# Decode of two attention and two MLP layers on one core: four streaming tasks in each window, ten behind it, and the chain's LayerNorms in fewer steps

## The chip, the core and the metric

The kernel runs on one core of one Trainium2 chip, as one launch. The metric is the device time in microseconds. A kernel is timed in several runs, and the median counts. A profile is taken of one further execution. Its own time and its span (first to last instruction) are given beside the median, because every duration below comes from that one execution. Engines are named as in the profile: PE (TensorE matmuls), PEld (its weight loads), DVE (VectorE), ACT (ScalarE), POOL (GpSimd) and SP (SyncE, which issues the loads here).

## The reference

Eight sequences (B = 8) decode one token each. A layer is attention over a cache of 8192 keys, with 32 query heads on 8 key/value heads of 128 elements, followed by an MLP of 512 x 1792. The same layer, with the same caches and weights, is applied twice.

```python
def _A_ref(x, k_cache, v_cache, wq, wo):
    q = (lambda x, *d: x.transpose(*d))((x @ wq).reshape(B, Sq, Hq, Dh), 0, 2, 1, 3)
    k = jnp.repeat(k_cache, rep, axis=1)
    v = jnp.repeat(v_cache, rep, axis=1)
    scores = jnp.einsum("bhqd,bhkd->bhqk", q, k) * (Dh ** -0.5)
    p = _softmax(scores, axis=-1)
    o = jnp.einsum("bhqk,bhkd->bhqd", p, v)
    return (lambda x, *d: x.transpose(*d))(o, 0, 2, 1, 3).reshape(B, Sq, Hq * Dh) @ wo
...
x = x + _A_ref(_layernorm(x, axis=-1), A_k_cache, A_v_cache, A_wq, A_wo)
x = x + _B_ref(_layernorm(x, axis=-1), B_w1, B_w2)
x = x + _A_ref(_layernorm(x, axis=-1), A_k_cache, A_v_cache, A_wq, A_wo)
x = x + _B_ref(_layernorm(x, axis=-1), B_w1, B_w2)
```

## The kernel before

**Tasks and granules.** A task is one key/value head of one sequence in one layer, (layer, b, g): 128 tasks. A task has four granules (`SPT`) of 2048 keys. For each granule one 512 KB load brings K and one brings V into the arena, which has 28 slots (`NSLOT`) of 512 KB. In iteration c of the main loop the kernel works on granule c. It transposes K on PE in two halves (L545), and ACT (L554) and DVE (L556) copy the halves back. It then computes the scores (L579). The product with V (L639) runs `LAG` = 6 granules later. The softmax is spread over the iterations by c modulo 4: `softmax_max` (DVE L590 and L592, POOL L594) at the end of iterations with remainder 3; `softmax_exp` (DVE L599 and L601, ACT L603) and then `softmax_sum` (DVE L609, POOL L611) in those with remainder 0 and 1; `emit_pt` (L619, L623) with remainder 1; the reciprocal (L628) with remainder 2.

**Kept heads.** The last 20 granules of K of a sequence (`KEEP`: heads 3 to 7) stay transposed in the arena from the first layer to the second, as do 3 granules of V (`KEEPV`); one granule of K is parked in PSUM. So a second-layer task of heads 3 to 7 loads V alone and transposes nothing. Heads 0 to 2 are free: they stream K and V in both layers.

**The order of the tasks** is laid by `make_tasks`. For each sequence b it takes the five kept heads of the first layer (`kept[b]`), then a window of free tasks (other sequences' heads 0 to 2, from `ahead` for the first layer and `behind` for the second), then the five kept heads of the second layer (`c[b]`), and at once `kept[b + 1]`. The windows have 6, 5, 5, 5, 5, 5, 5 and 6 tasks, 42 in all. From the end of `kept[b]` to `c[b]` the held K and V leave few slots for streaming.

**The loads.** `plan_loads` sorts all loads by the half step at which they are needed and gives each a slot and the half step after which that slot is free (`after`). SP issues them in that order, each when its slot has been released, by the scores for K (L579) or by the product with V (L639). Two neighbouring granules of a kept head are loaded as one 1 MB transfer if two neighbouring slots are free early enough. Before there are 199 such pairs and 442 single transfers, 641 in all.

**The chain.** When the last kept head of the first layer has been normalised, `chain_of(b)` lists what leads to the second layer's queries: the residual and first LayerNorm, the MLP, the second LayerNorm and the projection with `wq`. Its steps run one by one inside the iterations, at three places of the loop body: MID (after the copies of the transposed halves and the softmax steps, ahead of the product with V), TILE (PE work just ahead of the scores; in an iteration of a free task this comes after MID) and TURN (after the scores, ahead of `softmax_max`). At each place at most one step runs, and only if it is the next one and of that kind. The engines run their instructions in the order in which they are issued.

**A LayerNorm of the chain** has four parts in `ln_stages`. The first sums on DVE (L661) and across partitions on POOL (L663). The second (L669, L689, L690, POOL L692) sums the squares. The third (L708, L710, L698, L703) starts the reciprocal root. The fourth (L698, L703, L717) finishes it and writes the normalised column that PE reads next. In the chain the second and third are MID steps and the fourth is a TURN step, so that second, third with fourth, and the PE step behind them stand in three successive iterations.

In what follows w0, w1, ... are the granules of a window, counted from its first. As `LAG` is 6, the chain's first step comes in w6, whose remainder is 2. The chain before is: w6 `add_rest` and `met` (residual and first part), w7 second, w8 third and fourth, w9 `up`, w10 `expo` and `silu`, w11 and w12 `down`, w12 `gained` (residual and first part), w13 second, w14 third and fourth, w15 to w18 the queries (`ask` twice and `answer`, two times).

Of the kernel before, what the change touches and what calls it, by code (L numbers as in the profile page):

```python
# [17 lines left out]
KEEP = 20  # L18
KEEPV = 3
PARK = 1  # L20
LAG = 6
WIDE = 8
AHEAD = 8
# [114 lines left out]
def make_tasks(nb, nkv, keep_from):  # L138


    first = int(keep_from)
    a = [[(0, b, g) for g in range(first)] for b in range(nb)]
    kept = [[(0, b, g) for g in range(first, nkv)] for b in range(nb)]
    c = [[(1, b, g) for g in range(first, nkv)] for b in range(nb)]
    d = [[(1, b, g) for g in range(first)] for b in range(nb)]
    ahead = [t for b in range(1, nb) for t in a[b]]
    behind = []
    tasks = a[0] + kept[0]
    na = 0
    for b in range(nb):  # L150
        if b:
            tasks += kept[b]
        size = -(-(2 * first * (nb - 1)) // nb) if b in (0, nb - 1) else 2 * first * (nb - 1) // nb
        must = max(0, first * min(b + 1, nb - 1) - na)
        nd = size if b == nb - 1 else min(len(behind), first, size - must)
        tasks += behind[:nd]
        del behind[:nd]
        take = ahead[na:na + size - nd]
        na += len(take)
        tasks += take  # L160
        if b + 1 == nb:
            tasks += behind
        tasks += c[b]
        behind += d[b]
    tasks += d[nb - 1]
    assert na == len(ahead)
    return tasks

# [5 lines left out]
def plan_loads(tasks, kept, parked, keptv, nslot, ngran):  # L174

    single = set()
    while True:
        loads, copies = lay_loads(tasks, kept, parked, keptv, nslot, ngran, single)
        double = {rows_of(d, kept) for d in loads if d.n == 2}
        torn = {rows_of(d, kept) for d in loads if d.n == 1} & double  # L180
        if not torn:
            return loads, copies, double
        single |= torn
# [10 lines left out]
def lay_loads(tasks, kept, parked, keptv, nslot, ngran, single):  # L194
# [4 lines left out]
    for i, (layer, b, g) in enumerate(tasks):  # L199
        for k in range(ngran):  # L200
# [6 lines left out]
            if layer == 0 or (g, k) not in keptv:  # L207
                last = i if layer or (g, k) not in keptv else at[(1, b, g)]
                wanted.append(Load("V", layer, b, g, k, 2 * (c + LAG), 2 * (last * SPT + k + LAG)))
    wanted.sort(key=lambda d: (d.need, d.kind))  # L210
# [46 lines left out]
def _build(ctx, nc, A_x, A_k_cache, A_v_cache, A_wq, A_wo, B_w1, B_w2, out):  # L257
    B, _sq, D = A_x.shape
# [3 lines left out]
    REP = HQ // HKV  # L262
    KT = D // 128
# [9 lines left out]
    tasks = make_tasks(B, HKV, (len(order) - KEEP) // NGRAN)  # L273
    assert len(tasks) == 2 * B * HKV
    task_at = {t: i for i, t in enumerate(tasks)}
    parked = set(order[len(order) - PARK:])
    loads, copies, wide = plan_loads(tasks, kept, parked, keptv, NSLOT, NGRAN)
# [62 lines left out]
    mxp, nb, rs = [[few(1) for _ in range(NST)] for _ in range(3)]  # L340
# [27 lines left out]
    MISC = ps_bank("MISC")  # L368
    assert PARK == 1
    KEPTp = [ps_bank("KEPTp", BF16) for _ in range(HALVES)]  # L370
# [61 lines left out]
    with nc.Block() as block:  # L432

        @block.sync
        def _(sync_eng):
# [346 lines left out]
                )  # L782

            TILE, MID, TURN = range(3)

            def chain_of(b):
                x0, x1, x2 = [XT[n][:, :, b:b + 1] for n in range(3)]
                xn = one[2]
                qt2, rq2 = QT2[b % 2], f"QT2_{b % 2}"

                def attended():
                    sum_rows(x1, "XT1", x0, "XT0", 1.0)

                def up():
                    tiles([(t, xn[:, k, :], across(w1_sb[:, k, :], 0, FT)[:, t], k == 0, k == KT - 1)
                           for k in range(KT) for t in range(NT)], ["w1", "xn1"])

                hv = MISC[:, 0:FT * QR:QR]

                def expo():  # L800
                    upright(FT)
                    op(act, lambda: act.activation(eh, hv, ACT.Tanh, scale=0.5), reads=["MISC"], writes=["eh"])

                def silu():
                    op(dve, lambda: dve.scalar_tensor_tensor(hsT, eh, 1.0, hv, op0=ALU.add, op1=ALU.mult),
                       reads=["MISC", "eh"], writes=["hsT"])

                def down(q0, q1):
                    def run():
                        tiles([(t, hsT[:, q:q + 1], across(w2_sb[:, q, :], 0, KT)[:, t], q == 0, q == FT - 1)  # L810
                               for q in range(q0, q1) for t in range(NT)], all_of("w2") + ["hsT"])
                    return run

                AC = KB // QR

                def ask(a, k0, k1):
                    def run():
                        tiles([(t, xn[:, k, :], across(wq_sb[:, k, :], a * AC, (a + 1) * AC)[:, t],
                                k == 0, k == KT - 1) for k in range(k0, k1) for t in range(NT)], ["wq", "xn1"])
                    return run  # L820

                def answer(a):
                    def run():
                        upright(AC)
                        op(dve, lambda: dve.tensor_copy(qt2[:, a * AC:(a + 1) * AC], MISC[:, 0:KB:QR]),
                           reads=["MISC"], writes=[rq2])
                    return run

                n1, n2 = ln_stages(x1, "XT1", 1, one), ln_stages(x2, "XT2", 1, one)

                def gained():
                    sum_rows(x2, "XT2", x1, "XT1", 0.5)
                    n2[0]()

                def met():
                    attended()
                    n1[0]()

                return (
                    [(TURN, met), (MID, n1[1]), (MID, n1[2]), (TURN, n1[3])]  # L840
                    + [(TILE, up), (MID, expo), (TURN, silu), (TILE, down(0, FT // 2)), (TILE, down(FT // 2, FT))]
                    + [(TURN, gained), (MID, n2[1]), (MID, n2[2]), (TURN, n2[3])]
                    + [x for a in range(HQ // AC)
                       for x in ((TILE, ask(a, 0, KT // 2)), (TILE, ask(a, KT // 2, KT)), (TURN, answer(a)))]
                )

            def closing(n):
# [58 lines left out]
            def add_rest(b):  # L906
                while heads[b]:
                    add_heads(b)
# [33 lines left out]
            emit_q(0)  # L942

            chain = []
            chain_b = [None]
            turn = [0]
            last0 = {b: max(task_at[(0, b, g)] for g in range(HKV)) for b in range(B)}
            first1 = {b: min(task_at[(1, b, g)] for g in range(HKV)) * SPT for b in range(B)}
# [1 line left out]
            first = min(g for g, _k in kept)  # L950
# [16 lines left out]

            for c in range(NC + LAG):
                if c < NC:
                    layer, b, g, k = where(c)  # L970
                if c and c % SPT == 0 and c < NC:
                    assert layer == 0 or not chain or chain_b[0] != b
                    emit_q(c // SPT)
                ready = c < NC and (c < AHEAD or layer == 1 and (g, k) in kept)
                if ready:
                    scores(c)
                t = c + LEAD if c >= late - LEAD else c
                if not ready or t >= late:
                    emit_t(t, 0)
                    emit_t(t, 1)  # L980
                soft(c - SPT, softmax_exp)
                soft(c - SPT - 1, softmax_sum)
                soft(c - SPT - 2, softmax_rcp)
                step(MID)
                if 0 <= c - LAG:
                    emit_pv(c - LAG)
                    if (c - LAG) % SPT == SPT - 1:
                        emit_norm((c - LAG) // SPT)
                while copies and copies[0].need <= 2 * c:
                    emit_unpark(copies.pop(0))  # L990
                issue_until(2 * c)
                soft(c - SPT - 1, emit_pt)
                if turn[0] == B and not chain and heads[B]:
                    add_heads(B)
                if c < NC and not ready:
                    scores(c)
                issue_until(2 * c + 1)
                step(TURN)
                soft(c - SPT + 1, softmax_max)
                if c >= LAG and (c - LAG) % SPT == SPT - 1:  # L1000
                    tj = (c - LAG) // SPT
                    layer, b, g = tasks[tj]
                    if layer == 0:
                        heads[b].append(g)
                    elif b == B - 1:
                        heads[B].append(g)
                    if layer == 0 and tj == last0[b]:
                        assert not chain and turn[0] == b
                        chain.extend([(TILE, lambda b=b: add_rest(b))] + chain_of(b))
                        chain_b[0] = b  # L1010
                        turn[0] = b + 1
            assert not queue and not chain

            rest = closing(B)
# [37 lines left out]
```

## Time and profile before

| what | value |
|---|---|
| median of 3 runs | 1140.38 us (1137.9 to 1142.65) |
| the profiled execution | 1136.29 us |
| its span | 1134.5 us |
| busy PE / PEld / DVE / ACT / POOL | 935.0 / 698.9 / 558.3 / 491.0 / 117.3 us |
| loaded from HBM | 452.47 MB, 399 GB/s over the span |
| DMA engines busy | 9 tenths or more in 39 of 40 slices |
| single 512 KB loads: issue to landing, median | K 7.2 us, V 6.6 us |
| paired 1 MB loads: issue to landing, median | K 20.1 us, V 13.8 us |
| mean granted TensorE clock | 0.926 |

How to read it: the page gives sums over the whole span. The stages of the order above follow each other eight times, and a stage is read with the view of windows, which gives for each stretch of time the busy time of the engines, the granted clock, the share of time in which the DMA engines were busy, and the bytes per second. The timeline lists instructions in order of time: start, duration, engine, line, what it writes and reads, and in brackets the idle time before it with what ended it.

### The profile page before, as it was taken

What the parts mean: (1) busy time and instruction counts of PE and PEld (TensorE: products, weight loads), DVE (VectorE), ACT (ScalarE), POOL (GpSimd) and SP (SyncE); (2) the same over time, 40 slices, a digit from 0 to 9 for tenths busy, and PEclk for the clock granted to TensorE, in tenths of its full rate; (3) what the DMA queues carried; (4) which work ended last, traced back from release to release, by engine and by line L of the source; (5) the groups of instructions that cost most, each with busy time, mean ns of one, the idle gap of its engine ahead of it and who ended that gap; (6) DMA issues with size and microseconds to landing.
All of it is one profiled execution on the core that took longest, in us unless ns stands there. A gap on an engine that the chain in (4) does not pass through costs nothing.

```text
span 1134.5 us, 42794 instructions
## 1 busy us (share of the span) xinstructions
PE 935.0 (82%) x18792; PEld 698.9 (62%) x18792; DVE 558.3 (49%) x1710; ACT 491.0 (43%) x778; POOL 117.3 (10%) x300
## 2 busy tenths in 40 slices
PE   6687887888888888888888888888878888888796
PEld 4366664666566665666567665676566655665565
DVE  6444554445534553446444553446444553455444
ACT  5354442455335542554245542554245432554332
POOL 0000111001100101001100111001100111011010
PEclk9699998999879997999889997999789997999888
DMA  9999999999999999999999999999999999999995
GB/s 376 413 413 415 392 407 412 420 411 385 405 419 416 391 408 417 419 411 392 412 419 415 394 403 418 418 403 393 407 419 411 381 408 419 417 388 367 396 420 224
DMA packets 95550, 455.26 MB, mean 401 GB/s; under 512 B 10620, under 2 KB 10884, under 8 KB 69380
## 3 DMA queue, kind: packets, MB, share of 16 engines
q1 hardware_dynamic: 95348, 452.51, 99.1%
q8 instruction: 148, 2.42, 0.9%
q14 instruction: 38, 0.31, 0.1%
q10 hardware_dynamic: 16, 0.01, 0.0%
HBM read 452.47 MB, written 0.01 MB: 399 GB/s over the span
## 4 chain that ended last, share of the span: by engine, by line
DMA 40%; PE 37%; DVE 11%; ACT 5%; issue 5%; SPq 2%; POOL 0%; POOLq 0%; ACTq 0%; DVEq 0%
DMA arena<-in_A_v_cache_dram 32%; PE TPp L545 18%; PE SCp L579 9%; DVE arena L556 9%; DMA arena<-in_A_k_cache_dram 7%; PE OTp L639 4%; ACT arena L554 4%; PE TPp L619 2%; DMA wq<-in_A_wq_dram 2%; SPq L401 2%; PE MISC L754 2%; ACT P L603 1%; PE KEPTp L545 1%; DVE small L628 1%; DVE small L599 0%
## 5 line engine op out<-in xcount | busy, mean ns | idle before, releaser
L554 ACT COPY arena<-TPp 128x1024 bf16<-128x1024 bf16 x344 | 348.1, 1012 | 393.1 <-PE TPp L545 389.7
L545 PE MATMUL TPp<-ident,arena 128*128 128x128 bf16 x5504 | 377.8, 223 | 28.1 <-DMA arena<-in_A_k_cache_dram 22.3
L556 DVE COPY arena<-TPp 128x1024 bf16<-128x1024 bf16 x344 | 238.0, 692 | 329.7 <-PE TPp L545 327.0
L545 PEld LDWEIGHTS TPp<-ident,arena 128*128 128x128 bf16 x5504 | 317.9, 100 | 118.1 <-issue 62.1
L639 PE MATMUL OTp<-PT,arena 128*128 128x32 bf16 x8192 | 292.0, 179 | 56.6 <-DMA arena<-in_A_v_cache_dram 52.7
L639 PEld LDWEIGHTS OTp<-PT,arena 128*128 128x128 bf16 x8192 | 252.6, 97 | 136.0 <-DMA arena<-in_A_v_cache_dram 105.7
L579 PE MATMUL SCp<-arena,QB 128*32 128x512 bf16 x2048 | 223.8, 429 | 71.5 <-DVE arena L556 24.0
L603 ACT ACTIVATE P<-SCp,small 128x512 bf16<-128x512 f32 x128 | 87.9, 687 | 203.5 <-DVE small L601 157.8
L590 DVE TENSOR_REDUCE small<-SCp 128x1 f32<-128x512 f32 x128 | 88.5, 692 | 103.7 <-PE SCp L579 102.5
L579 PEld LDWEIGHTS SCp<-arena,QB 128*32 128x32 bf16 x2048 | 59.8, 96 | 112.5 <-ACT arena L554 53.4
L594 POOL PARTITION_ALL_REDUCE small<-small x128 | 47.5, 371 | 620.9 <-DVE small L592 620.9
L611 POOL PARTITION_ALL_REDUCE small<-small x128 | 55.2, 431 | 332.4 <-DVE at L653 146.5
L619 PE MATMUL TPp<-ident,P 128*128 128x128 bf16 x512 | 54.9, 235 | 26.4 <-ACT arena L554 14.6
L619 PEld LDWEIGHTS TPp<-ident,P 128*128 128x128 bf16 x512 | 31.5, 103 | 35.5 <-ACT arena L554 20.1
L623 DVE COPY PT<-TPp 128x256 bf16<-128x256 bf16 x128 | 37.3, 291 | 20.8 <-PE TPp L619 18.9
L609 DVE TENSOR_SCALAR small<-small 128x4 f32<-128x4 f32 x128 | 28.7, 224 | 37.9 <-ACT P L603 37.9
L592 DVE TENSOR_SCALAR small<-small 128x4 f32<-128x4 f32 x128 | 29.4, 229 | 4.5
L599 DVE TENSOR_TENSOR small<-small 128x4 f32<-128x4 f32 x128 | 20.0, 157 | 20.9 <-POOL small L594 20.9
L767 DVE STREAM_TRANSPOSE MISC<-MISC 128x128 f32<-128x128 f32 (+2 forms) x40 | 22.1, 552 | 10.0 <-PE MISC L754 10.0
L754 PE MATMUL MISC<-wo,at 128*32 128x128 bf16 x1024 | 26.0, 231 | 0.0
L603 ACT ACTIVATION_READ_ACCUMULATOR P<-SCp,small 128x1 f32 x128 | 24.7, 193 | 0.0
L601 DVE TENSOR_REDUCE small<-small 128x1 f32<-128x4 f32 x128 | 20.1, 157 | 4.4
(102 smaller groups left out, 329.7 us busy)
## 6 DMA issues: line engine op xcount, KB each, us to landing
arena<-in_A_v_cache_dram SPq DMA_DIRECT2D x131, 1024.0 KB, 13.8
arena<-in_A_v_cache_dram SPq DMA_DIRECT2D x226, 512.0 KB, 6.6
arena<-in_A_k_cache_dram SPq DMA_DIRECT2D x216, 512.0 KB, 7.2
arena<-in_A_k_cache_dram SPq DMA_DIRECT2D x68, 1024.0 KB, 20.1
arena<-in_A_wo_dram SPq DMA_DIRECT2D x8, 512.0 KB, 12.7
wq<-in_A_wq_dram SPq DMA_DIRECT2D x1, 4096.0 KB, 24.8
w<-in_B_w_dram SPq DMA_DIRECT2D x1, 1792.0 KB, 22.3
arena<-in_B_w_dram SPq DMA_DIRECT2D x3, 512.0 KB, 16.9
```

The lines of the kernel that those rows point to most:

```text
L545: lambda c=c: pe.transpose(tpv[:, c, :], chunk(slot, h * GRP + c), ident[:, :])
L554: op(act, lambda: act.copy(dst, bank[:, :]), reads=[rt], writes=[r_half(slot, h)])
L556: op(dve, lambda: dve.tensor_copy(dst, bank[:, :]), reads=[rt], writes=[r_half(slot, h)])
L579: lambda t=t: pe.matmul(SCp[bank][t * QR:(t + 1) * QR, :], QB[qn][:, NGRAN - 1 - k:NGRAN - 1 - k + QR], keys[:, t * KB:(t + 1) * KB], star ...
L590: op(dve, lambda: dve.tensor_reduce(mxp[st][:, :], SCp[bank][:, :], AX.X, ALU.max), reads=[f"SC{bank}"], writes=[f"mxp{st}"])
L594: op(pool, lambda: pool.partition_all_reduce(mxa[st][:, :], mxr[st][:, :], 128, bass.bass_isa.ReduceOp.max), reads=[f"mxr{st}"], writes=[f ...
L603: op(act, lambda: act.activation(P[:, :], SCp[bank][:, :], ACT.Exp, bias=nb[st][:, 0:1], scale=SM_SCALE, accum_out=rs[st][:, :]), reads=[f ...
L611: op(pool, lambda: pool.partition_all_reduce(ssa[st][:, :], ssm[st][:, :], 128, bass.bass_isa.ReduceOp.add), reads=[f"ssm{st}"], writes=[f ...
L619: lambda c=c: pe.transpose(tpv[:, c, :], P[:, c * 128:(c + 1) * 128], ident[:, :])
L623: op(dve, lambda: dve.tensor_copy(PT[:, :, :, :], tpv.rearrange("p c (t q) -> p c t q", q=QR)[:, :, :, 0:NGRAN * REP]), reads=[f"TP{tb}"], ...
L639: lambda n=n, cc=cc: pe.matmul(otp, chunk(slot, n), PT[:, cc % CPB, (cc // CPB) % NT, cc // (CPB * NT)::NGRAN].unsqueeze(2).to_broadcast([ ...
L754: lambda t=t, col=col, w=w, start=start, stop=stop: pe.matmul(MISC[t * QR:(t + 1) * QR, 0:math.prod(w.shape[1:])], spread(col), w, start=s ...
```

## The change

The window has four tasks (`WINDOW`) for every b but the last, where it takes what is left of `behind`, which is four too. The other ten free tasks go behind `c[b]`, ahead of `kept[b + 1]`: 1, 1, 2, 1, 2, 1 and 2 of them. A function `put` takes tasks from `behind` first, as far as the first-layer tasks that are due allow it. By the planner's own rules the new order has 187 paired and 466 single loads, 653 in all, for the same bytes.

In the chain the third part of both LayerNorms becomes a TURN step and the fourth a MID step. So the second and third stand in one iteration, and the fourth stands in the same iteration as the PE step that reads it. The chain is then: w6 `add_rest` and `met`, w7 second and third, w8 fourth and `up`, w9 `expo` and `silu`, w10 and w11 `down`, w11 `gained`, w12 second and third, w13 fourth and the first `ask`, w14 `ask` and `answer`, w15 `ask`, and the last `ask` and `answer` in the first granule of `c[b]`. A list `asked` counts the queries that are there, and the assertion ahead of `emit_q` asks for those of the task's head instead of an empty chain.

```diff
--- before.py
+++ after.py
@@ -18,6 +18,7 @@
 KEEP = 20
 KEEPV = 3
 PARK = 1
+WINDOW = 4
 LAG = 6
 WIDE = 8
 AHEAD = 8
@@ -147,22 +148,27 @@
     behind = []
     tasks = a[0] + kept[0]
     na = 0
+    rest = 2 * len(ahead) - nb * WINDOW
+
+    def put(size, must):
+        nonlocal na, tasks
+        nd = max(0, min(len(behind), size - max(0, must - na)))
+        tasks += behind[:nd]
+        del behind[:nd]
+        tasks += ahead[na:na + size - nd]
+        na += len(ahead[na:na + size - nd])
+
     for b in range(nb):
         if b:
             tasks += kept[b]
-        size = -(-(2 * first * (nb - 1)) // nb) if b in (0, nb - 1) else 2 * first * (nb - 1) // nb
-        must = max(0, first * min(b + 1, nb - 1) - na)
-        nd = size if b == nb - 1 else min(len(behind), first, size - must)
-        tasks += behind[:nd]
-        del behind[:nd]
-        take = ahead[na:na + size - nd]
-        na += len(take)
-        tasks += take
-        if b + 1 == nb:
-            tasks += behind
+        gap = rest * (b + 1) // (nb - 1) - rest * b // (nb - 1) if b + 1 < nb else 0
+        due = first * min(b + 1, nb - 1)
+        put(WINDOW if b + 1 < nb else len(behind), due - gap)
         tasks += c[b]
         behind += d[b]
-    tasks += d[nb - 1]
+        if b + 1 < nb:
+            put(gap, due)
+    tasks += behind
     assert na == len(ahead)
     return tasks
 
@@ -782,6 +788,7 @@
                 )
 
             TILE, MID, TURN = range(3)
+            asked = [0] * B
 
             def chain_of(b):
                 x0, x1, x2 = [XT[n][:, :, b:b + 1] for n in range(3)]
@@ -836,12 +843,18 @@
                     attended()
                     n1[0]()
 
+                def answered(a):
+                    def run():
+                        answer(a)()
+                        asked[b] = (a + 1) * AC
+                    return run
+
                 return (
-                    [(TURN, met), (MID, n1[1]), (MID, n1[2]), (TURN, n1[3])]
+                    [(TURN, met), (MID, n1[1]), (TURN, n1[2]), (MID, n1[3])]
                     + [(TILE, up), (MID, expo), (TURN, silu), (TILE, down(0, FT // 2)), (TILE, down(FT // 2, FT))]
-                    + [(TURN, gained), (MID, n2[1]), (MID, n2[2]), (TURN, n2[3])]
+                    + [(TURN, gained), (MID, n2[1]), (TURN, n2[2]), (MID, n2[3])]
                     + [x for a in range(HQ // AC)
-                       for x in ((TILE, ask(a, 0, KT // 2)), (TILE, ask(a, KT // 2, KT)), (TURN, answer(a)))]
+                       for x in ((TILE, ask(a, 0, KT // 2)), (TILE, ask(a, KT // 2, KT)), (TURN, answered(a)))]
                 )
 
             def closing(n):
@@ -942,7 +955,6 @@
             emit_q(0)
 
             chain = []
-            chain_b = [None]
             turn = [0]
             last0 = {b: max(task_at[(0, b, g)] for g in range(HKV)) for b in range(B)}
             first1 = {b: min(task_at[(1, b, g)] for g in range(HKV)) * SPT for b in range(B)}
@@ -969,7 +981,7 @@
                 if c < NC:
                     layer, b, g, k = where(c)
                 if c and c % SPT == 0 and c < NC:
-                    assert layer == 0 or not chain or chain_b[0] != b
+                    assert layer == 0 or asked[b] >= (g + 1) * REP
                     emit_q(c // SPT)
                 ready = c < NC and (c < AHEAD or layer == 1 and (g, k) in kept)
                 if ready:
@@ -1007,7 +1019,6 @@
                     if layer == 0 and tj == last0[b]:
                         assert not chain and turn[0] == b
                         chain.extend([(TILE, lambda b=b: add_rest(b))] + chain_of(b))
-                        chain_b[0] = b
                         turn[0] = b + 1
             assert not queue and not chain
 
```

## The prediction

> **What bounds the kernel now.** I read the page's slices first (DMA busy in nine tenths of nearly every slice, PE 82%), then the view of windows over one round of the order, then SP's own waits, then the timeline of the chain's first LayerNorm. The windows, in order: `kept[2]`; the window of sequence 2 (w0 to w19, here sequence 1's second layer among its tasks); `c[2]`; two pieces of that window; the last window; a piece of it. The columns end with PE's granted clock, DMA share, GB/s.
>
> ```profile
> core 0: us, PE busy (x) PEld busy (x) DVE busy (x) ACT busy (x) POOL busy (x), PEclk, DMA share, GB/s
> 328.19:375.28 47.09, 40.16 (x829) 32.81 (x821) 22.25 (x60) 24.12 (x35) 4.00 (x10) 0.97 1.02 416
> 375.28:422.67 47.39, 40.91 (x845) 31.30 (x848) 27.70 (x88) 23.80 (x35) 5.24 (x13) 1.00 1.01 398
> 422.67:452.90 30.23, 23.88 (x472) 14.64 (x468) 12.44 (x46) 7.05 (x19) 4.37 (x11) 0.77 1.02 417
> 388.00:398.00 10.00, 8.63 (x196) 6.72 (x194) 6.76 (x25) 4.79 (x7) 1.61 (x4) 1.00 0.97 364
> 398.00:422.00 24.00, 20.99 (x439) 15.46 (x436) 14.84 (x46) 11.88 (x17) 2.40 (x6) 1.00 1.03 407
> 1002.90:1064.45 61.55, 50.47 (x992) 37.88 (x996) 32.24 (x100) 28.72 (x42) 6.05 (x15) 0.97 0.99 377
> 1021.00:1034.00 13.00, 10.68 (x220) 7.67 (x221) 6.61 (x24) 5.15 (x9) 0.81 (x2) 0.87 0.92 334
> ```
>
> The transfers bound the kernel: 452.5 MB must come in, and the stages differ only by a few per cent in rate. The window loads in singles and runs at 407 once it has settled (398 to 422); the stages with pairs run at 416 to 417. The one real loss in a window is a dip of about 10 us near w5 to w9: 10 x (1 - 364/407) = 1.06 us. In the last window it grew: one granule's scores began 5.6 us after the one before (1021.32 to 1026.91), where a granule with `up` elsewhere takes 3.4 (393.70 to 397.06 below). PE had waited 1.47 us for K and its clock fell. That granule was 2.2 us late, and DMA lost 13 x (1 - 334/407) = 2.3 us. So in w8 lateness of PE becomes lateness of the loads one to one. The reason is in SP's waits inside sequence 2's window:
>
> ```profile
> SPq L87 <- PE OTp L639: 19.1, 15, 1.9
> SPq L87 <- PE SCp L579: 12.9, 17, 2.0
> ```
>
> SP spends 32 of 47 us waiting for PE to release a slot. A late PE issues late loads.
>
> Now the LayerNorm in w7 and w8 (L590 is `softmax_max` of w7; L556 at 392.86 the copy of w8; L708 to L717 third and fourth part; L754 is `up`, in w9):
>
> ```profile
> 391.58 0.16 DVE L690 TENSOR_REDUCE small<-small 128x1 f32<-128x4 f32 x1
> 391.83 0.40 POOL L692 PARTITION_ALL_REDUCE small<-small  x1 [1.33 <-DVE small L690]
> 391.87 0.69 DVE L590 TENSOR_REDUCE small<-SCp 128x1 f32<-128x512 f32 x1
> 392.71 0.57 PE L639 MATMUL OTp<-PT,arena 128*128 128x32 bf16 x16
> 392.86 0.69 DVE L556 COPY arena<-TPp 128x1024 bf16<-128x1024 bf16 x1
> 393.70 0.40 PE L579 MATMUL SCp<-arena,QB 128*32 128x512 bf16 x4 [0.42 <-DVE small L599]
> 393.73 0.14 DVE L708 TENSOR_SCALAR small<-small 128x1 f32<-128x1 f32 x1
> ...
> 394.55 0.22 DVE L698 SCALAR_TENSOR_TENSOR small<-small 128x1 f32<-128x1 f32 x1
> ...
> 395.00 0.16 DVE L717 TENSOR_TENSOR tiny<-small 128x4 bf16<-128x4 f32 x1
> 395.13 0.69 DVE L556 COPY arena<-TPp 128x1024 bf16<-128x1024 bf16 x1
> ...
> 396.30 0.94 PE L754 MATMUL MISC<-w,tiny 128*32 128x448 bf16 x16
> ...
> 397.06 0.39 PE L579 MATMUL SCp<-arena,QB 128*32 128x512 bf16 x4
> ```
>
> The reader is to see that DVE has hardly a gap from w7's maximum to w8's copy, that the third part sits behind that copy, where its sum has long been there, and that `up` waits for nobody, a granule later.
>
> **The change, part by part.**
>
> *First LayerNorm, new wait.* The third part now stands ahead of `softmax_max` in w7. Its sum comes from POOL at 392.23, so DVE, in order, waits from 391.74 to about 392.26. The third part takes 0.82 us (393.73 to 394.55) and ends near 393.08. Queued behind it are the maximum (at 393.10 instead of 391.87, 1.23 late), then w8's copy, for which w8's scores wait, then the softmax steps, then the fourth part: 393.73 + 1.23 = 394.96, plus 0.61 (394.55 to 395.16) = 395.57. `up`, now in w8, reads that result. PE has finished w8's product with V at 393.28, so it idles 2.3 us where it idled 0.42. `up` holds the scores for 0.76 us (396.30 to 397.06), so w8's scores come at 396.4 instead of 393.70; w9 no longer holds `up` and follows 2.3 us later, the spacing of the two copies L556 (395.13 - 392.86), at 398.7 instead of 397.06. Net: PE, and every slot it releases, is 1.6 us late.
>
> *Second LayerNorm.* `gained` now shares w11 with `softmax_max`: its DVE work (about 0.7 us, 389.28 to 390.02 where `met` does the same) goes ahead of the maximum, some 0.6 late. In w12 DVE carries the copy (0.61), two softmax steps (0.26), the second part (0.55), the wait for POOL (0.52) and the third part (0.82): 2.76 against a period of 2.27, 0.5 late. In w13 the first `ask` waits for copy, L609 and fourth part (0.61 + 0.22 + 0.61 = 1.44 after the copy's start, where `up` began 1.17 after it): 0.3 late. Together 1.4 us, in three pieces.
>
> *What of it DMA loses.* Upper end, one to one as in the last window. Lower end: from 398 to 422 the rate stays at 407 although the `ask` granules lengthen PE's path by some 0.7 us each (PE waited 0.47 us for V even at 395.57), so pieces up to 0.7 can be absorbed. First LayerNorm 0.9 to 1.6, value 1.3 (nearest row: the last window's 2.2, in the same granule); second 0 to 1.4, value 0.4. Per window 1.7; eight windows (each sequence has a chain): **+13.6 us**, between 7.2 and 24.
>
> A rule of the Trainium skill bears on the size. The last window's 2.3 us contain a fallen clock (0.87), there after a wait of 1.47 us. "TensorE: Matmul & The Clock Gate", section "What's actually happening", lets the clock fall only after an idle window of about 3.4 us; by that an idle of 2.3 us costs no clock. The trace shows a fall beside a shorter wait; by it another 0.7 us (2.2 late less 1.47 waited) could come in each window, 5.6 in all, which stands with the third rival.
>
> *Ten tasks out of the tight stage.* 42 window tasks become 32, and 10 x 4 x 1.05 MB = 41.9 MB move where slots abound. The later part of a window, which is what gets shorter, already runs at 407, the pace of singles; from 376 to 388, ahead of the dip, it was 406. So the saving is near 0. If the whole difference between 398 and 416 were due to the tight slots, it would be 41,900 x (1/398 - 1/416) = 4.6 us. Value -1.
>
> *The dip.* It follows the kept heads, whose K is not released, and all eight windows still follow those. Free tasks ahead of `kept` take PE 2.27 us a granule, less than their 1.05 MB take at 417 (2.51), so PE arrives with less in stock and more in flight. Bounds: 0, and seven dips gone (-7.4). Value -1.
>
> *Pairs.* Twelve pairs become singles: 12.6 MB at 407 for 417, +0.7 us. The twelve further issues on SP are hidden by its 32 us of waiting; without that they would cost 12 x 0.33 = 4 us.
>
> *No cost:* `asked` and the planner run at build time; instruction counts on PE, DVE, ACT and POOL stay. The queries for the first head of `c[b]` are answered in w14, one granule ahead of need, with some 2 us cover; without it `c[b]` would wait that much once a window.
>
> **Sum**: 13.6 - 1 - 1 + 0.7 = +12.3 us. The span goes from 1134.5 to 1146.8. The profiled execution (1136.29) lies 4.1 below the median; the same step on the median gives 1140.38 + 12.3 = **1152.7**.
>
> **Rivals.**
>
> 1. *The lateness is absorbed.* If the transfers in flight (407 GB/s x 6.6 us / 524 KB = 5) cover all but 0.3 us a window: 2.4 - 2 + 0.7 = +1.1, **1141.5**. For it: the steady 407. Against it: 0.92 and 334 in the last window.
>
> 2. *Faster: the tight stage was the price.* With less in stock the dips vanish (-7.4), the shorter window saves its upper bound (-4.6), and lateness costs 0.5 a window (+4.0) and the pairs 0.7: -7.3, **1133**. It wins from the point where a window loses less than 1.4 us to the chain. For it: 416 wherever slots abound. Against it: the dip lies at the window's front, which stays.
>
> 3. *Lateness in full.* 3.0 us a window without absorption, or 1.6 with the clock's fall and part of the second: 24 + 0.7 - 2 = +23, **1163**. For it: the one row with such a delay. Against it: it needs the second LayerNorm's small pieces to count too.
>
> 4. *Splitting costs per transfer.* Two K singles one after the other (2 x 7.2) against a pair of V (13.8) give at most 0.6 us for each split: 12 x 0.6 = 7.2 for the 0.7 above, **1159**. Against it: singles alone hold 407 of 417. The Trainium skill, "DMA: Bandwidth & Descriptors", section "Anatomy of one DMA — SWDGE (gpsimd) path", fits a fixed 2.0 us to every DMA issued that way; by it twelve more would add an estimated 24 us if nothing overlapped. The trace, whose loads come from SP, does not agree: 407 with singles alone leaves no room for 2 us on each.
>
> That the change does not do what it says is unlikely: the loads fit their slots by the planner's rules and the chain's steps fall as counted.
>
> **How the numbers follow.** Chances: forecast 0.53, absorbed 0.24, faster 0.12, in full 0.08, splitting 0.03. The likeliest one's own range is 1144 to 1161. To leave out no more than 2 in 10 the range reaches down into the absorbed and the faster case and up to the full one: **1136 to 1164**. A measurement of this kernel tells about 0.5% (5.7 us) from no change: faster than 1134.7 about 0.10 (most of rival 2); slower than 1146.1: 0.46 of the forecast, 0.08, 0.03 and a little of rival 1, 0.59; the rest, 0.31, within.
>
> **What would show it.** In the changed profile, L754 should appear waiting for DVE's L717, twice in each sequence; L708 for POOL's L692; the copies of w8 about 1.2 us later; windows at some 380 to 390 GB/s with a second dip behind w8; the stages with free slots at 416 as before. I am wrong on the mechanism if no PE wait of about 2 us stands ahead of `up`; wrong on its price if it stands there and the windows still run at 395 or more.

## The result, and the profile after

| | before | after |
|---|---|---|
| median | 1140.38 us (1137.9 to 1142.65) | 1155.47 us (1154.29 to 1156.72) |
| profiled execution, its span | 1136.29, 1134.5 us | 1156.72, 1154.9 us |
| busy PE / DVE / ACT | 935.0 / 558.3 / 491.0 us | 928.5 / 553.4 / 492.2 us |
| loaded, rate over the span | 452.47 MB, 399 GB/s | 452.47 MB, 392 GB/s |

The changed kernel takes 1.0135 times as long (95% interval 1.0116 to 1.0153), 15 us more. No engine has more work; the same bytes come in more slowly. Where, the view of windows shows: sequence 2's window (w0 to w15), sequence 5's, and two pieces of the first. The last columns are PE's granted clock, DMA share and GB/s.

```profile
369.41:411.28 41.87, 35.11 (x697) 26.39 (x700) 21.86 (x75) 18.89 (x28) 4.45 (x11) 0.96 0.96 353
774.90:816.80 41.90, 35.17 (x700) 26.28 (x700) 21.98 (x75) 18.88 (x28) 4.45 (x11) 0.96 0.98 363
378.00:388.00 10.00, 8.53 (x186) 6.66 (x182) 5.87 (x23) 5.27 (x8) 1.43 (x4) 1.00 0.98 350
388.00:400.00 12.00, 9.62 (x188) 6.83 (x188) 5.70 (x20) 4.10 (x7) 1.19 (x3) 0.86 0.89 313
```

Sequence 2's window ran at 398 GB/s before and runs at 353 now. The old dip is still there (378 to 388), and behind it stands a second, deeper one (388 to 400 at 313), where before the same 12 us of the window (393.88 to 405.88) ran at 402. The time that a window loses can be read off as its length x (1 - rate/407). Over the eight windows this gives 13.9 us before and 32.9 us after, 19.0 more, against 20.4 more in the span. So the windows hold nearly the whole loss of these two executions. (The medians lie only 15 us apart: the execution profiled before was 4.1 us under its median.)

SP's own waits in that window, of after:

```profile
SPq L88 <- PE SCp L585: 15.4, 16, 3.3
SPq L88 <- PE OTp L645: 14.4, 11, 2.8
```

The longest single wait for a slot has grown from 2.0 to 3.3 us. What makes PE release it late is in the timeline of w7 and w8 (L596 is `softmax_max`, L714 to L723 the third and fourth part, L760 `up`; lines have moved by six, in the LayerNorm also):

```profile
385.70 0.16 DVE L696 TENSOR_REDUCE small<-small 128x1 f32<-128x4 f32 x1
385.95 0.40 POOL L698 PARTITION_ALL_REDUCE small<-small  x1 [1.28 <-DVE small L696]
...
386.38 0.15 DVE L714 TENSOR_SCALAR small<-small 128x1 f32<-128x1 f32 x1 [0.53 <-POOL small L698]
...
387.09 0.68 DVE L596 TENSOR_REDUCE small<-SCp 128x1 f32<-128x512 f32 x1
...
387.95 0.69 DVE L562 COPY arena<-TPp 128x1024 bf16<-128x1024 bf16 x1
...
389.25 0.16 DVE L723 TENSOR_TENSOR tiny<-small 128x4 bf16<-128x4 f32 x1
389.47 1.62 PE L760 MATMUL MISC<-w,tiny 128*32 128x448 bf16 x16 [1.68 <-DVE tiny L723]
...
390.87 0.65 PE L585 MATMUL SCp<-arena,QB 128*32 128x512 bf16 x4
```

DVE waits 0.53 us for POOL, the maximum comes 1.39 us after L696 (before: 0.29), and PE stands still for 1.68 us ahead of `up`. Then `up` itself takes 1.62 us where it took 0.94, beside a fallen clock (0.86 over those 12 us). Over the whole kernel the view of the tile `tiny` counts who waited for it:

```profile
who waited for it (us, times):
  PEld MISC L760: 17.4, 15
  PE MISC L760: 16.8, 16
```

Sixteen waits of PE, two for each sequence. The list of waits before had none of them.

### The profile page after: what moved, and what is told of

Its sections match the earlier page's. It is cut to its first block, busy times and chain, and to the rows that moved or that the text cites. A ratio compares the mean times of both kernels' runs of the same rounds, so it can differ in the third digit from the quotient of the medians.

```text
span 1154.9 us, 42793 instructions
## 1 busy us (share of the span) xinstructions
PE 928.5 (80%) x18792; PEld 699.2 (61%) x18792; DVE 553.4 (48%) x1710; ACT 492.2 (43%) x778; POOL 117.8 (10%) x300
## 3 DMA queue, kind: packets, MB, share of 16 engines
HBM read 452.47 MB, written 0.01 MB: 392 GB/s over the span
## 4 chain that ended last, share of the span: by engine, by line
DMA 52%; PE 29%; DVE 8%; ACT 4%; issue 4%; SPq 1%; POOL 0%; POOLq 0%; ACTq 0%; DVEq 0%
DMA arena<-in_A_v_cache_dram 31%; DMA arena<-in_A_k_cache_dram 19%; PE TPp L551 14%; PE SCp L585 6%; DVE arena L562 5%; PE OTp L645 4%; ACT arena L560 3%; PE MISC L760 3%; DMA wq<-in_A_wq_dram 2%; PE TPp L625 2%; SPq L407 1%; ACT P L609 1%; DVE small L596 0%; DVE small L709 0%; PE MISC L732 0%
## 5 line engine op out<-in xcount | busy, mean ns | idle before, releaser
L585 PE MATMUL SCp<-arena,QB 128*32 128x512 bf16 x2048 | 220.9, 422 | 69.3 <-DVE arena L562 28.9
L596 DVE TENSOR_REDUCE small<-SCp 128x1 f32<-128x512 f32 x128 | 88.4, 690 | 95.8 <-PE SCp L585 95.7
L760 PE MATMUL MISC<-w,tiny 128*32 128x128 bf16 (+1 forms) x576 | 19.7, 274 | 13.4 <-DVE tiny L723 13.4
L760 PE MATMUL MISC<-wo,at 128*32 128x128 bf16 x1024 | 24.6, 221 | 0.0
```

Of the source, the lines that this page charges most:

```text
L585: lambda t=t: pe.matmul(SCp[bank][t * QR:(t + 1) * QR, :], QB[qn][:, NGRAN - 1 - k:NGRAN - 1 - k + QR], keys[:, t * KB:(t + 1) * KB], star ...
L596: op(dve, lambda: dve.tensor_reduce(mxp[st][:, :], SCp[bank][:, :], AX.X, ALU.max), reads=[f"SC{bank}"], writes=[f"mxp{st}"])
L760: lambda t=t, col=col, w=w, start=start, stop=stop: pe.matmul(MISC[t * QR:(t + 1) * QR, 0:math.prod(w.shape[1:])], spread(col), w, start=s ...
```

## The experiments

All ratios are against the kernel before, run on the same chip as the kernel named.

| run | ratio (95% interval) | median us |
|---|---|---|
| changed kernel | 1.0135 (1.0116 to 1.0153) | 1155.47 |
| e1, new LayerNorm steps, old order | 1.0202 (1.0177 to 1.0227) | 1161.95 |
| e2, first LayerNorm's steps old | 1.0031 (1.0011 to 1.0050) | 1143.00 |
| e3, second LayerNorm's steps old | 1.0155 (1.0136 to 1.0175) | 1157.73 |
| e4, windows of five, both old | 1.0022 (1.0000 to 1.0044) | 1143.88 |
| e5, no LayerNorms, old order | 1.0006 (0.9979 to 1.0032) | 1141.81 |
| e6, no LayerNorms, changed order | 0.9934 (0.9910 to 0.9957) | 1134.22 |
| e9, `up` a granule later | 1.0083 (1.0055 to 1.0112) | 1150.55 |
| e10, root whole in w8 | 1.0123 (1.0081 to 1.0164) | 1154.61 |
| e11, scaled late | 1.0030 (1.0007 to 1.0052) | 1145.02 |
| e12, scaled late, answers spread | 0.9966 (0.9940 to 0.9992) | 1138.84 |
| e13, as e11, old order | 1.0027 (1.0004 to 1.0051) | 1144.62 |
| e14, as e12, old order | 1.0065 (1.0036 to 1.0095) | 1146.43 |

The theory on trial is lateness: PE's wait inside the chain makes the loads late. Its rival is that the order of the tasks (shorter windows, tasks behind `c`, fewer pairs) is the price.

**The two halves of the change, one at a time.** e1 puts the new steps into the old order:

```diff
-                    [(TURN, met), (MID, n1[1]), (MID, n1[2]), (TURN, n1[3])]
+                    [(TURN, met), (MID, n1[1]), (TURN, n1[2]), (MID, n1[3])]
...
-                    + [(TURN, gained), (MID, n2[1]), (MID, n2[2]), (TURN, n2[3])]
+                    + [(TURN, gained), (MID, n2[1]), (TURN, n2[2]), (MID, n2[3])]
```

> The kernel before with only the LayerNorm steps changed (third part a TURN step, fourth a MID step, in both LayerNorms); the order of the tasks is the old one. Lateness theory (PE's wait ahead of `up` and the first `ask` is the price): about 13 us for the first LayerNorm and 4 for the second, so 1152 to 1157 us, with windows of 380 to 388 GB/s. Order theory (the shorter window, the tasks behind `c` and the lost pairs are the price): within 3 us of 1140.

Two of its windows (sequences 2 and 5; in the old order these are 20 granules):

```profile
385.20:434.40 49.20, 41.11 (x845) 31.37 (x848) 27.08 (x88) 23.81 (x35) 5.26 (x13) 1.00 0.99 375
769.60:820.20 50.60, 42.70 (x844) 32.22 (x848) 27.09 (x88) 23.81 (x35) 5.26 (x13) 0.97 0.99 367
```

The steps alone cost 2.0%, about 23 us: more than the whole change, and more than expected. By the window sum its eight windows lose 38.3 us, 24.4 more than before, against 24.8 in the span. So lateness holds, and the order must be giving something back. e5 and e6 measure that. In both, `up` reads x1 and `ask` reads x2, unnormalised, and the LayerNorms are left out; e6 has the same edits in the changed kernel.

```diff
-                    [(TURN, met), (MID, n1[1]), (MID, n1[2]), (TURN, n1[3])]
+                    [(TURN, met)]
...
-                tiles([(t, xn[:, k, :], across(w1_sb[:, k, :], 0, FT)[:, t], k == 0, k == KT - 1)
+                tiles([(t, x1[:, k, :], across(w1_sb[:, k, :], 0, FT)[:, t], k == 0, k == KT - 1)
```

> The kernel before without the chain's two LayerNorms: `up` reads the residual x1 and `ask` the residual x2, unnormalised, and all four parts of both LayerNorms are left out. It serves as the base for the next run. Every theory: 1134 to 1140 us, since the LayerNorms before made PE wait little.

> The changed kernel without the chain's two LayerNorms, in the same way (`up` reads x1, `ask` reads x2, unnormalised). What differs from the run before it is the order of the tasks and the pairs alone. Lateness theory: the order is worth about nothing, within 3 us of the run without LayerNorms in the old order. Order theory: about 10 us slower than that run. A gain hidden by the chain's waits (the shorter window as such pays): 4 us or more faster than it.

Windows of sequences 2 and 5, first e5, then e6:

```profile
377.62:425.27 47.65, 41.50 (x844) 31.48 (x848) 24.37 (x66) 23.68 (x35) 3.63 (x9) 1.00 1.01 395
757.67:806.84 49.17, 41.89 (x845) 31.32 (x848) 24.37 (x66) 23.69 (x35) 3.63 (x9) 1.00 1.00 381
```

```profile
363.70:401.80 38.10, 33.68 (x702) 25.25 (x700) 19.75 (x53) 18.32 (x28) 2.83 (x7) 1.00 1.02 396
762.70:801.20 38.50, 34.05 (x700) 25.98 (x700) 19.64 (x53) 17.98 (x26) 2.83 (x7) 0.97 1.00 384
```

The third branch came true: the order pays, 0.72% or some 8 us. The eight windows last 408.8 us in e5 and 306.6 in e6, and their losses are 20.1 and 11.7 us, a difference of 8.4 against 8.9 in the span. Of it 5.0 us stand in the later part of the windows, from 23 us after their start (6.1 us lost in 225 against 1.1 in 123), and 3.0 in the dips ahead of it (13.6 against 10.6): there is less window, and what is left of it runs a little faster. Each profile is a single execution, though: the window sum before is 13.9, and that of e5, which takes the same time at the median, 20.1. The old LayerNorm steps cost nothing measurable (e5). With the new steps the order is worth the same (1.0135 against 1.0202), and the new steps cost the same in both orders: 1.0202 / 1 and 1.0135 / 0.9934 = 1.0202. The change is the sum of a gain of 8 us and a loss of 23.

e4 leaves nearly all of both out: windows of five tasks, old steps.

```diff
-WINDOW = 4
+WINDOW = 5
```

> The changed planner with windows of five tasks instead of four (two tasks instead of ten behind `c`), and both LayerNorms' steps as before; 190 pairs instead of 199. Lateness theory: no new wait, so the time before, 1138 to 1142 us. Order theory (a price on tasks behind `c`): two tenths of 15 us, 1143.

It came out 0.2% slower, at the edge of its interval: above the range of lateness and near the 1143 of the order theory, though a fifth of the order's gain would make it 0.14% faster. Nine of the twelve pairs are already split in it, so a price of the pairs may be hidden here; no run separates it.

**Which LayerNorm.** e2 and e3 each give one of them its old steps back (the first pair of lines above, reversed; the second pair, reversed).

> The changed kernel with the first LayerNorm's steps as before (second and third MID, fourth TURN), the second as changed; the order of the tasks stays the changed one, and the first queries are answered one granule later, in w15. Lateness theory: the wait ahead of `up` is gone and with it about 12 us, 1142 to 1146 us. Order theory: stays at 1152 to 1156.

> The changed kernel with the second LayerNorm's steps as before, the first as changed. Lateness theory: the large piece is the first LayerNorm's, in the dip, so only 3 to 5 us come back, 1150 to 1153 us. If the two LayerNorms weigh the same per us of PE's wait: about 8 us back, 1147. Order theory: 1152 to 1156.

e2 came as lateness has it: 1.04% or 12 us back. e3 missed all three numbers; it got no faster. Its list of waits gives a reason:

```profile
ACT QB L576 <- DVE QT L832: 26.5, 16, 1.8
PE MISC L760 <- DVE tiny L723: 12.4, 8, 1.8
PE MISC L760 <- DVE QT L832: 6.4, 8, 0.8
```

The eight waits for the second LayerNorm are gone (16.8 to 12.4 us), but the chain is one granule longer and the first answer falls in w15. At the start of `c[b]` ACT's copy of the queries waits for it, and so does PE, with the next `ask`, behind which the first scores stand. The changed kernel's list has neither of these waits on L832. So 4.4 us of PE's waits went and 6.4 came. e2 has the same new waits (5.8 us of PE's), so its 12 us understate the first LayerNorm.

**Which part of the wait.** In w7 and w8 two things are new: the third part delays w8's copy, and `up` waits for the fourth. e9 keeps the first alone, e10 the second alone.

```diff
-                    [(TURN, met), (MID, n1[1]), (TURN, n1[2]), (MID, n1[3])]
+                    [(TURN, met), (MID, n1[1]), (TURN, n1[2]), (MID, n1[3]), (TILE, lambda: None)]
```

> The changed kernel with an empty TILE step between the first LayerNorm's fourth part and `up`: the third part still stands ahead of `softmax_max` in w7 and delays w8's copy by 1.1 us, but `up` comes in w9 and waits for nobody. If PE's wait for the fourth part is the price: as with the old steps of the first LayerNorm, 1142 to 1145 us. If the late copy alone already carries it: 1150 or more. Between them, by what pieces up to 0.7 us absorb: 1145 to 1149.

```diff
-                    [(TURN, met), (MID, n1[1]), (TURN, n1[2]), (MID, n1[3])]
+                    [(TURN, met), (MID, n1[1]), (MID, rooted)]
...
+                def rooted():
+                    n1[2]()
+                    n1[3]()
```

> The changed kernel with the first LayerNorm's third and fourth part together as one MID step in w8, ahead of `up`: DVE does not wait for POOL in w7 and w8's copy is not delayed, but `up` still waits for the fourth part, some 1.9 us instead of 2.3. If PE's wait is the price: 1150 to 1154 us. If DVE's wait for POOL and the late copy are: 1142 to 1146.

PE in w7 and w8 of e9:

```profile
384.56 0.40 PE L585 MATMUL SCp<-arena,QB 128*32 128x512 bf16 x4 [0.48 <-DVE small L675]
...
387.79 0.40 PE L585 MATMUL SCp<-arena,QB 128*32 128x512 bf16 x4 [1.43 <-DVE small L605]
```

The late copy alone holds w8's scores 0.95 us longer than w7's. e9 stands 0.5% (6 us) above e2, which has the same answer in w15 and no late copy, and 0.5% below the changed kernel, which has its answer in w14. e10, with no late copy and PE's wait nearly whole, is as slow as the changed kernel within its interval. So PE's wait suffices for nearly the whole loss, and the late copy by itself for a part of it; the two are not additive, because PE waits for the later of them.

**Taking the wait away.** If the order pays and the waits cost, a chain without waits should beat both kernels. In e11 the second part writes the centred column at once, `up` and `ask` read that, the root runs beside them, and its result scales what leaves PE:

```diff
+                    if n == 1:
+                        op(dve, lambda: dve.scalar_tensor_tensor(
+                            xnv, s1a[:, 0:n].unsqueeze(1).to_broadcast([128, KT, n]), -1.0 / D, xv, op0=ALU.mult, op1=ALU.add),
+                           reads=["s1a", rx], writes=[rxn])
...
-                    op(act, lambda: act.activation(eh, hv, ACT.Tanh, scale=0.5), reads=["MISC"], writes=["eh"])
+                    op(dve, lambda: dve.scalar_tensor_tensor(
+                        eh, hv, 0.5, yr[:, 0:1].to_broadcast([128, FT]), op0=ALU.mult, op1=ALU.mult),
+                       reads=["MISC", "yr"], writes=["eh"])
+                    op(act, lambda: act.activation(th, eh, ACT.Tanh), reads=["eh"], writes=["th"])
...
+                    [(TURN, met), (MID, n1[1]), (TILE, up), (MID, root(n1)), (MID, expo), (TURN, silu)]
+                    + [(TILE, down(0, FT // 2)), (TILE, down(FT // 2, FT)), (TURN, gained), (MID, n2[1])]
+                    + [(TILE, ask(0, 0, KT // 2)), (MID, root(n2)), (TILE, ask(0, KT // 2, KT)), (TURN, answered(0))]
```

e12 adds an empty TURN step ahead of `answered(0)`; e13 and e14 are e11 and e12 in the old order.

> The changed order of the tasks, with a chain in which PE never waits for the root: `up` and `ask` read the centred column as soon as the second part has it (in w7 and w12), the root runs beside them as one MID step, and its result scales what comes out of PE (in `expo` and `answer`). If the order pays by itself (7.5 us faster without LayerNorms) and PE's waits were all that turned it into a loss: 1133 to 1138 us, 3 to 7 us under the kernel before. If DVE's added work beside the copies costs as much as the late copy did: 1142 or more.

> The same with an empty TURN step ahead of the first `answer`, so that its transpose falls in w14 instead of w13, where DVE has the softmax's copy and the root already. If DVE's load in one iteration matters: 1 to 3 us under the run without it. If not: equal within 2 us.

> The same chain as in the run that scales late, in the old order of the tasks. If the order pays by itself: 5 to 8 us slower than with the changed order, about the time of the kernel before, 1139 to 1143 us. If the gain is the chain's: within 2 us of it.

> The chain that scales late and spreads the answers (the fastest so far), in the old order of the tasks. Between the two orders with the same chain lies then the order alone, in kernels that compute the reference. If the order pays by itself: 4 to 7 us slower than with the changed order, 1142 to 1146 us. If the gain of that run was the chain's: 1137 to 1140 us.

e11 missed its first range: 1145, in the branch of DVE's load. The trace shows another reason, again the start of `c[b]`, now for the second answer, which falls in w15 and writes the same tile:

```profile
405.58 0.23 DVE L835 TENSOR_SCALAR QT<-MISC,small 128x16 bf16<-128x16 f32 x1
405.74 0.68 DVE L596 TENSOR_REDUCE small<-SCp 128x1 f32<-128x512 f32 x1
405.85 0.20 ACT L576 COPY QB<-QT 128x4 bf16<-128x4 bf16 x1 [1.42 <-DVE QT L835]
406.10 0.10 PEld L585 LDWEIGHTS SCp<-arena,QB 128*32 128x32 bf16 x4 [1.30 <-ACT QB L576]
406.11 0.40 PE L585 MATMUL SCp<-arena,QB 128*32 128x512 bf16 x4 [1.00 <-ACT QB L576]
```

PE stands some 1.0 us there, in every window. In e12 the second answer falls in the first granule of `c[b]` and the copy for its first head is ahead of it; the wait is gone, and e12 is 6.2 us faster than e11. (Its empty step also spreads DVE's load, which was expected to give 3 us at most; the two are not separated.) It beats both kernels: 0.34% under before, 1.7% under the change.

The same chain in the old order (e14) is 1.0065, so the order is worth 1% here, or 0.6% if e13 is taken as the base; the intervals of e13 and e14 overlap. Against e11, e13 came within 2 us, as its second branch has it, but e11 has the wait at `c[b]` and e13's list has none. The late scaling by itself gains nothing: in the old order it is 0.3 to 0.65% slower than the old chain. What it gives is a chain that fits the short window with little waiting.

PE at `up` (in w7 here) and at the first `ask` in e12, where the changed kernel waited 1.68 us ahead of `up`:

```profile
382.44 0.94 PE L760 MATMUL MISC<-w,tiny 128*32 128x448 bf16 x16
...
395.57 0.61 PE L760 MATMUL MISC<-wq,tiny 128*32 128x512 bf16 x8 [0.62 <-DVE tiny L694]
```

## Why the prediction was right, and where its terms were not

The forecast was +12.3 us, and +15.1 was measured. The direction, the place and the mechanism were right. Two terms were wrong, in opposite directions: the loss was some 9 us larger than foretold and the order's gain some 7. That the sum came so near is in part luck.

*The wait.* Foretold: DVE's maximum 1.23 us late, w8's copy as much, PE's idle ahead of `up` 2.3 us; measured in sequence 2: 1.1 late (1.39 against 0.29), the copy right behind it, idle 1.68 (1.57 to 2.13 over the eight). PE waits twice in each sequence and a second dip stands behind w8, as foretold; the windows run at 340 to 385 GB/s, where 380 to 390 was foretold.

*What DMA loses by it: mis-sized.* "Per window 1.7; eight windows: +13.6 us". The steps cost 2.0%, 23 us, near the upper bound of 24. The windows ran at 368, 378, 353, 371, 375, 363, 340 and 385 GB/s; by the window sum they lose 4.1 us each, where e6's lose 1.5. Two things that the 1.7 leaves out stand in the traces.

One is the clock. The rule that a short idle costs no clock was weighed, and its side taken for the sum; the row of the last window, which spoke against it, was right. In five of the eight windows the clock fell to half behind `up`, and these lose 4.9 us each, the other three (the second, fifth and eighth) 2.7. But the step is smaller elsewhere: 5.1 (six windows) against 3.9 (two) in e1, 3.7 (five) against 3.4 (three) in e3, 4.8 (four) against 4.1 (four) in e10. So the fall goes along with 0.3 to 2.2 us a window; over five windows that is some 2 to 11 of the 21 us that the eight lose more than e6's.

The other is an echo: in seven of the eight windows PE stands still once more, 0.6 to 1.6 us, for K or V that comes late, 10 to 14 us behind the start of `up`. In sequence 2, where no wait of PE in the window was over 0.5 us before:

```profile
400.51 1.07 PE L551 MATMUL TPp<-ident,arena 128*128 128x128 bf16 x16 [1.39 <-DMA arena<-in_A_k_cache_dram]
```

In the fifth and the seventh window the clock fell behind this second wait, too. What the clock and the echo each cost was not tried alone and stays open. The rule of the Trainium skill in "TensorE: Matmul & The Clock Gate", section "What's actually happening" (a fall only after some 3.4 us of idle), does not fit these runs, where it fell behind 1.57 to 2.13 us.

*The order: mis-sized.* "The saving is near 0. Value -1", "The dip. Value -1", pairs +0.7: -1.3 in sum. Measured -8 (e5 and e6), -7.5 (e1 and the change), -7 to -11 (e12 with e13 and e14). The step that failed was to read the late part of one window (407 in sequence 2) for all. From 23 us after their start the windows of the kernel before ran at 397 to 408, but the last at 376, and those of e5, a slower execution, at 387 to 405. That gives 5.0 of the 8.4 us between e5 and e6; why the dips, too, lose less there stays open. The two bounds given, -4.6 and -7.4, together hold it. Rival 2 had this right and lost all the same, because lateness cost 23, not 4.

*The second LayerNorm: not measured alone.* 0.4 us a window was taken, between 0 and 1.4. e3 removed eight of the sixteen waits (4.4 us in sum) and brought in the new wait at `c[b]` (6.4 us).

*Pairs and SP's issues.* No run separates them; e6's gain of 8 us is net of all twelve split pairs. If e4's 2.5 us and the missing fifth of the gain, 1.6 us, were the price of its nine split pairs, one would cost an estimated 0.45 us, not far from rival 4's 0.6. So that term is not excluded, but the slowdown does not need it: e1 keeps all 199 pairs and has the whole loss.

*Queries one granule ahead of need.* The cover was real: where an experiment took it away (e2, e3, e9, e11), `c[b]` waited.

## What to carry to other kernels

Where a stage lives on few free slots, a wait of the compute engine is paid in transfer time (here 16.8 us of PE's waits came with 23 us of loss), and moving a dependent pair of steps into one iteration buys such a wait; look first at what stands behind the moved instruction on its in-order engine. A change of two parts should be measured by its parts: here a gain of 8 us lay under a loss of 23, and taking most of the wait out (read the centred column, scale afterwards) turned the whole into a small gain, 0.34%. When a chain is shortened, check its far end too: a wait of 0.8 to 1 us came back at the first consumer in four of the experiments.

## What the runs showed of the hardware that was not expected

PE's clock fell to half after idles far shorter than the 3.4 us for which it stayed there. Three stretches of 3.4 us behind `up` in the changed kernel, with the granted clock as third column from the right:

```profile
389.60:393.00 3.40, 3.40 (x35) 2.07 (x28) 0.00 (x0) 0.59 (x3) 0.00 (x0) 0.50 0.91 335
656.60:660.00 3.40, 3.14 (x60) 2.09 (x60) 1.25 (x3) 1.21 (x3) 0.33 (x1) 1.00 0.97 366
1066.20:1069.60 3.40, 3.13 (x60) 2.13 (x60) 1.20 (x3) 1.26 (x3) 0.28 (x1) 1.00 0.99 389
```

After 1.68 us of idle the clock was 0.50 for 3.4 us, and `up` took 1.62 us; after 1.57 us (656.56) it stayed at 1.00, and `up` took 0.94. Over the eight windows it fell behind 1.57, 1.61, 1.65, 1.68 and 2.13 us and stayed behind 1.57, 1.60 and 1.61: the length of the idle alone does not decide it.
